# A gated attention + SSM kernel: V's and the gate's weights on GpSimd's DMA queue, and another hand-tuned order

## The chip, the cores and the metric

The kernel runs on one core of a Trainium2 chip. The core has five engines that run their own instruction streams in order and meet at semaphores: TensorE (PE, matrix multiplications), VectorE (DVE), ScalarE (ACT), GpSimd (POOL) and SyncE (SP, here only an issuer of DMAs). ACT and POOL can issue DMAs too; an engine that issues a DMA does nothing else for that long. The metric is the time of one execution in microseconds (us); several executions are made, and the median is taken.

## The reference

Two branches on the same input `x` (2048 tokens of 448 values), mixed by a gate:

```python
g = sigmoid((x * gate_w).sum(-1, keepdims=True))
a = attention(x, wq, wk, wv, wo)     # 16 query heads of 28, ONE key and value head, no mask
b = ssm_conv(x, A_re, A_im, B_re, B_im, C_re, C_im, log_dt, Dskip)
return g * a + (1 - g) * b
```

Attention: `q = x wq` (16 heads of 28), `k = x wk` and `v = x wv` (one head of 28 for all), softmax of `q k^T / sqrt(28)` over all 2048 keys, times `v`, all heads joined times `wo`. That makes 16 x 2048 x 2048 exponentials. The SSM branch builds, for every one of 448 channels, a kernel `K[l] = Re sum_n C dB exp(dt A l)` over 256 complex modes and 2048 places, convolves the channel with it causally, and adds `x * Dskip`. All inputs are bfloat16.

## The kernel before

**Attention.** Queries are worked in 16 units `i` (4 blocks of 512 queries times 4 groups of 4 heads), and each unit has 64 tiles of 128 keys x 512 queries, so there are 1024 tiles. Tiles go in sets of three and two alternately (sets `s`, 410 in all). For each set TensorE computes scores into banks of PSUM (`qk`), ScalarE takes the exponential of the whole set at once (L1357) into a ring `expT` of 15 tiles, and TensorE multiplies four tiles at a time by the values (`pv`, L1383), into the bank `psB`. Scores come in two forms: `row` (L1323) reads `qT`, the query as projected, and puts tiles of different heads in different 32-row groups of the array; `full` (L1332) reads `qM`, a copy of the query with zeros between the heads, which a DMA from POOL's queue writes. Sets below 10, and from 12 on those of three tiles, use the row form. `qproj` projects the next unit's queries, `norm` divides by the softmax's sum, `outp` and `fold` multiply by `wo` and the gate and add into `O`. A shift of the scores keeps the exponentials in range; it comes from the largest key and query magnitudes (`km`, `kap`, `Wb`), so the first score waits for all keys.

**Prologue.** `x` comes in four quarters in the order `QO` = 0, 3, 1, 2. Quarters 0 and 3 are loaded as they are, transposed on TensorE (L718) and copied from PSUM by ACT (L728) or VectorE (L730), as the list `XA` of (quarter, piece) says; quarters 1 and 2 (`DQ`) come in by a transposing DMA, so entries of `XA` for them have no effect. For each quarter four matmuls (L736) make the keys, VectorE takes their largest magnitude (`km`, L742), and the eviction into `kT` is made by VectorE (L746) for quarters in `KD`, else by ACT (L750). V and the gate are one matmul group per 128 tokens (L763) with the weights `Wv`, which VectorE copies (L645, L647) from the staging tile `seedw`; V's and the gate's weights land there by four DMAs of the ACT queue. K's weights and `log_dt` come by the ACT queue too, all others by SP. In the same time ACT and VectorE make the seeds of the SSM tables from A (L862 to L919), for which ACT needs three table loads (exp, sin, exp again).

**SSM branch.** VectorE makes tables (`masters`, `tables`), TensorE makes kernels from them (`kgen`, L1095), VectorE evicts them, POOL's queue writes them to DRAM (`KP`), SP loads them back as Toeplitz tiles (`tload`, L1131), and TensorE convolves (`conv`, L1155), with VectorE (L1170), TensorE (L1181) and VectorE (L1189) adding the result into `O`. There are 28 convolutions. This fills the time of VectorE and what the scores and PV leave of TensorE.

**What sets the order.** The class `Prog` records all operations with an estimated duration, and `schedule` builds the order of each engine's instructions before the kernel is emitted: of the ready operations it takes the earliest, then the one with the smaller `pr`, then the older. Up to the first exponential (`goal`) an operation on a longer path to it goes first, if it makes the other wait for no more than `HEAD` of its duration; `RANK` adds nanoseconds to single operations' path lengths, by number. `ISSUE` is the assumed time of one DMA issue by queue, `extra` an addition to a DMA's assumed landing. An operation with `pr` of 2 or more is assumed ready later by `SLACK`. `idle` puts filler matmuls (L1398, which add zeros into `psB`) into planned gaps of TensorE within the times `FILL`, as long as the planned work of the last `SPAN` ns is below `LOW` of it. Engines run in this order on the chip, whatever arrives first.

## Time and profile before

| | |
|---|---|
| median of 3 runs | 506.75 us (506.19 to 508.49) |
| the profiled execution | 507.17 us, of which the span from first to last instruction is 505.3 us |
| ACT, DVE, PE, POOL busy | 482.6, 455.0, 448.2, 165.3 us |
| exponentials of scores (L1357) | 410, 466.2 us; idle before them 5.8 us |
| first exponential starts | 22.89 us |
| last exponential ends | 495.41 us |
| filler matmuls (L1398) | 36, 0.39 us each, from 40.8 to 392.7 us |
| granted TensorE clock, mean | 0.985 |

In a timeline line the first number is the start in us from the span's start, the second the time taken, then engine, line, operation, tile written, tile read, shapes and count, and in brackets the engine's idle time before it and what ended that. `SPq`, `ACTq` and `POOL ... DMA` lines are issues of DMAs. In a group line the numbers behind the bar are busy time, mean ns of one, and idle time before them with what ended most of it. A line of stretches gives, for a start and an end in us, the length and the busy time and count of PE, PEld, DVE, ACT and POOL, then the granted clock, the DMA engines' busy share and GB/s.

### The profile page before, as it was taken

To read this page: it belongs to the slowest core of one execution; us is meant where nothing else is said; L and a number is where in the kernel's file an instruction comes from. 1 tells how busy PE (TensorE), PEld (TensorE's weight loads), DVE (VectorE), ACT (ScalarE), POOL (GpSimd) and SP (SyncE) were. 2 spreads that over 40 slices of the span, in tenths; PEclk is the share of its full clock that TensorE was granted. 3 is DMA by queue.
4 is the path that set the end of the run, shared out by engine and by line. 5 is a ranking of instruction groups with operands and counts; after the bars stand their busy time and mean duration, and the time that the engine had idled before them with its cause. 6 is when DMAs were issued, how large, how long until landed. Compare 5 with 4: busy or idle time off the path is not lost.

```text
span 505.3 us, 18926 instructions
## 1 busy us (share of the span) xinstructions
PE 448.2 (89%) x8469; PEld 195.1 (39%) x8469; DVE 455.0 (90%) x834; ACT 482.6 (96%) x432; POOL 165.3 (33%) x308
## 2 busy tenths in 40 slices
PE   6797778898998999989898899999899999999885
PEld 2322213343433434334433344344343444344453
DVE  6899999999999999999999999999999999922334
ACT  5899999999999999999999999999999999999892
POOL 8533224252143520615332321435232152451000
PEclk8889999999999999999999999999999999999899
DMA  9977901979949797999989999599999979899982
GB/s 188 224 210 129 59 22 50 340 226 365 363 153 332 244 317 250 269 361 324 366 282 371 318 317 362 199 339 369 356 283 345 369 233 384 264 358 369 385 302 47
DMA packets 123395, 139.51 MB, mean 276 GB/s; under 512 B 56169, under 2 KB 63370, under 8 KB 123314
## 3 DMA queue, kind: packets, MB, share of 16 engines
q1 hardware_dynamic: 112208, 128.89, 79.8%
q0 software_dynamic: 8656, 9.25, 6.7%
q8 instruction: 66, 1.08, 0.9%
q10 hardware_dynamic: 2450, 0.17, 0.4%
q14 instruction: 15, 0.12, 0.1%
HBM read 125.18 MB, written 5.22 MB: 258 GB/s over the span
## 4 chain that ended last, share of the span: by engine, by line
ACT 48%; DVE 38%; PE 10%; issue 2%; DMA 1%; SPq 1%
ACT expT L1357 48%; DVE tab L1048 5%; DVE tab L1059 3%; DVE tab L1060 3%; DVE msq L991 3%; DVE tab L1070 2%; DVE tab L1058 2%; DVE tab L1057 2%; DVE mbf L1011 2%; PE psS L1332 2%; PE psB L1383 2%; DVE seedz L995 2%; PE psS L1323 2%; DVE seedz L993 1%; DVE tmp L1066 1%
## 5 line engine op out<-in xcount | busy, mean ns | idle before, releaser
L1357 ACT ACTIVATE expT<-psS 128x1536 bf16<-128x1536 f32 (+1 forms) x410 | 466.2, 1332 | 5.8 <-PE psS L1323 2.7
L1332 PE MATMUL psS<-qM,kT 128*128 128x512 bf16 (+2 forms) x455 | 122.5, 360 | 13.8 <-ACT expT L1357 10.5
L1383 PE MATMUL psB<-expT,vaug 128*32 128x512 bf16 (+2 forms) x1152 | 103.4, 366 | 3.1 <-issue 2.0
L1323 PE MATMUL psS<-qT,kT 29*128 29x512 bf16 (+2 forms) x699 | 82.1, 362 | 22.9 <-ACT expT L1357 21.5
L154 POOL DMA_DIRECT2D KP_scratch<-kstg x112 | 61.1, 553 | 65.6 <-DVE kstg L1110 37.4
L1048 DVE TENSOR_TENSOR tab<-tab,mbf 128x512 bf16<-128x512 bf16 (+3 forms) x56 | 64.6, 1154 | 0.0
L1383 PEld LDWEIGHTS psB<-expT,vaug 128*32 128x32 bf16 x1152 | 27.6, 93 | 76.1 <-issue 71.2
L154 POOL DMA_DIRECT2D rdenB<-R_scratch x56 | 28.4, 513 | 62.6 <-DMA R_scratch<-denT 53.7
L1332 PEld LDWEIGHTS psS<-qM,kT 128*128 128x128 bf16 x455 | 28.4, 97 | 50.7 <-ACT expT L1357 33.3
L1323 PEld LDWEIGHTS psS<-qT,kT 29*128 29x128 bf16 x699 | 21.4, 91 | 67.4 <-ACT expT L1357 53.6
L154 POOL DMA_DIRECT2D qM<-qT x64 | 32.2, 511 | 37.8 <-DVE qT L966 22.1
L1059 DVE TENSOR_TENSOR tab<-tab 128x1024 bf16<-128x1024 bf16 (+4 forms) x70 | 41.6, 595 | 0.0
L1060 DVE TENSOR_TENSOR tab<-tab 128x128 bf16<-128x128 bf16 (+4 forms) x70 | 41.5, 594 | 0.0
L1155 PE MATMUL psS<-T,U 128*32 128x128 bf16 (+3 forms) x1504 | 35.3, 220 | 0.3 <-DVE qT L966 0.3
L154 POOL DMA_DIRECT2D denT<-acc x14 | 10.0, 715 | 74.8 <-DVE kstg L1106 37.1
L1070 DVE TENSOR_TENSOR tab<-tab,tmp 128x4096 bf16<-128x4096 bf16 x14 | 32.0, 2285 | 0.1
L1058 DVE TENSOR_TENSOR tab<-tab,mbf 128x4096 bf16<-128x4096 bf16 x14 | 31.9, 2279 | 0.0
L1057 DVE TENSOR_TENSOR tab<-tab,mbf 128x4096 bf16<-128x4096 bf16 x14 | 31.9, 2276 | 0.0
L1155 PEld LDWEIGHTS psS<-T,U 128*32 128x32 bf16 (+3 forms) x1504 | 24.9, 94 | 13.8 <-issue 9.4
L1155 PE MATMUL psX<-T,U 128*32 128x128 bf16 (+7 forms) x1216 | 28.8, 222 | 0.1
L991 DVE TENSOR_TENSOR msq<-seedz 128x384 f32<-128x384 f32 (+1 forms) x50 | 27.1, 542 | 0.2
L1066 DVE TENSOR_TENSOR tmp<-tmp,mq 128x64 bf16<-128x64 bf16 (+4 forms) x70 | 25.3, 362 | 0.1
(160 smaller groups left out, 544.2 us busy)
## 6 DMA issues: line engine op xcount, KB each, us to landing
T<-KP_scratch SPq DMA_DIRECT2D x170, 512.0 KB, 9.1
U<-KP_scratch SPq DMA_DIRECT2D x40, 512.0 KB, 9.6
tab<-KP_scratch SPq DMA_DIRECT2D x14, 512.0 KB, 10.9
rdenB<-R_scratch POOLq DMA_DIRECT2D x56, 64.0 KB, 5.5
qM<-qT POOLq DMA_DIRECT2D x64, 32.0 KB, 5.1
tab<-in_A_x_dram SPq DMA_DIRECT2D x8, 224.0 KB, 3.6
O<-cst SPq DMA_DIRECT2D x1, 1792.0 KB, 9.9
KP_scratch<-kstg POOLq DMA_DIRECT2D x112, 16.0 KB, 4.1
```

Of the source, the lines that this page charges most:

```text
L154: return [e.dma_start(o, i, **kw) for o, i in pairs]
L991: pg.op("dve", lambda e: e.tensor_tensor(m2(msq), z2, z2, ALU.mult), el(2 * n), rd=[kr, ki] + first, wr=["msq"], pr=pr)
L1048: vo(lambda e, dst=dst, src=src, mri=mri: e.tensor_tensor(dst, src, mri, ALU.mult), 4 * n, done + mk(lv), [kr, ki, tk])
L1057: vo(lambda e, src=src, mi=mi, tv=tv: e.tensor_tensor(tv, src, mi, ALU.mult), 2 * n, done + mk(lv), [tk])
L1059: vo(lambda e, dc=dc, tc=tc: e.tensor_tensor(dc[0], dc[0], tc[1], ALU.subtract), n, [tk, kr], [kr])
L1060: vo(lambda e, dc=dc, tc=tc: e.tensor_tensor(dc[1], dc[1], tc[0], ALU.add), n, [tk, ki], [ki])
L1070: vo(lambda e: e.tensor_tensor(tab.v(0, P, FM, [[4, 1024], [1, 4]]), tab.v(0, P, lo + 124, [[CG, 32], [-4, 32], [1, 4]]), rho.v(0, P, 0, [ ...
L1155: r = e.matmul(ps.v(32 * j, 32 - 2 * n, 128 * k, [[1, 128]]), self.U.v(0, P, (4 * gi + j) * 32 + 2 * n, [[1, 32 - 2 * n]]), tbuf.v(0, P, t ...
L1323: r = e.matmul(self.psS.v(0, P, 512 * b + o, [[1, n]]), kT.v(32 * h, DH + 1, 128 * kt, [[1, 128]]), qT.v(32 * h, DH + 1, 512 * (i % 2) + q ...
L1332: r = e.matmul(self.psS.v(0, P, 512 * b + o, [[1, n]]), kT.v(0, P, 128 * kt, [[1, 128]]), self.qM.v(0, P, (i % 2) * XQ + 512 * h + qo, [[1 ...
L1357: pg.op("act", lambda e: e.activation(expT.v(0, P, 512 * es[0], spread(es, n)), self.psS.v(0, P, 512 * bs[0], spread(bs, n)), AF.Exp, scal ...
L1383: r = e.matmul(self.psB.v(32 * h, 32, qo, [[1, n]]), vaug.v(0, P, 32 * kt, [[1, 32]]), expT.v(0, P, 512 * ring[t] + o, [[1, n]]), start=(k ...
```

## The change

- V's weights (`wv`) and the gate's (`wg`), two DMAs each, are issued by POOL instead of ACT.
- `XA`: ACT copies pieces 1 and 3 of quarter 0 (before 1, 2, 3) and 0, 1, 2 of quarter 3 (before all four); VectorE copies the rest.
- `KD`: the keys of quarter 2 are evicted by VectorE and those of quarter 1 by ACT (before the other way round).
- Set 10 takes its scores in the row form instead of the full form.
- Numbers of the planner: `HEAD`, `RANK`, the issue time of an ACT DMA, the assumed landing of early, transposing, `wq`, `wv`, `wg` and `kw` DMAs, the fillers' bound `LOW` and last time in `FILL`, the priorities of later query projections (1.5 for 1.58), of the last two convolutions' matmuls (1.3 for 1.6) and of the last units' `norm_last` (0.9 for 1.5 and 2). They issue no instruction; the order of all engines is built from them.

```diff
--- before.py
+++ after.py
@@ -36,8 +36,8 @@
 TW = 4 * 1024
 XQ = NT * 512
 SIN2PI = 6.2831850
-XA = ((0, 1), (0, 2), (0, 3), (1, 0), (2, 2), (2, 3), (3, 0), (3, 1), (3, 2), (3, 3))
-KD = (0, 1, 3)
+XA = ((0, 1), (0, 3), (1, 0), (1, 1), (1, 2), (2, 3), (3, 0), (3, 1), (3, 2))
+KD = (0, 2, 3)
 GX = 3
 DQ = (1, 2)
 VNS = 140
@@ -85,16 +85,16 @@
 class Prog:
     SEM_NS = 56
     DMA_NS = 2200
-    ISSUE = {"pool": 540.0, "sp": 470.0, "act": 470.0}
+    ISSUE = {"pool": 540.0, "sp": 470.0, "act": 700.0}
     LAT = {"pe": 170.0, "act": 173.0, "dve": 82.0, "pool": 85.0, "sp": 60.0}
     SAME = {"act": 100.0, "dve": 125.0, "pool": 150.0}
     SWITCH = 105.0
     BLOCK, FIRST, FETCH, IDLE, NEED = 256, 192, 5900.0, 3300.0, .015
     HALF = (21000.0, 21000.0, 1.8)
-    HEAD = 0.6
-    RANK = {111: 3000, 62: 3000, 39: -6000, 20: -3000, 30: -6000, 190: -6000, 46: -6000, 29: 700, 65: -6000, 84: 6000, 195: 6000, 40: -6000, 38: 3000, 33: 6000}
+    HEAD = 0.4
+    RANK = {111: 3000, 190: -6000, 29: -6000, 38: -6000, 43: 3000, 23: -1500, 41: -3000, 192: -6000, 82: -1500, 153: -6000, 27: -3000, 118: 1500, 37: 1500, 150: -6000, 105: 3000, 39: -6000, 74: -1500, 92: 3000}
     POOL = (7,)
-    LOW, SPAN, FILL = .53, 3413.0, (36000.0, 440000.0)
+    LOW, SPAN, FILL = .45, 3413.0, (36000.0, 490000.0)
     AHEAD = 1500.0
     SLACK = {"pe": 700.0, "dve": 150.0}
 
@@ -157,7 +157,7 @@
         if cost is None:
             cost = nd * ns / 16.0 * (1.15 if size < 1500 else 1.0 if nd >= 512 else 1.4 if size < 3000 else 1.25)
         o = self.op(eng, fn, cost, rd, wr, pr)
-        o.slot, o.ndma, o.extra = slot, len(pairs), extra + 200 * (early or flip)
+        o.slot, o.ndma, o.extra = slot, len(pairs), extra + 500 * (early or flip)
         o.iss = len(pairs) * (1400.0 if flip else 640.0 if early else self.ISSUE[eng])
         prev = self.slots.get(slot)
         if prev is not None:
@@ -626,12 +626,12 @@
         lx(QO[1])
         lraw(1)
         lraw(0)
-        pg.dma(rows(wst, 0, ins["A_wq"], D), (448, 896), "wq", wr=["wqs"], cost=1500)
+        pg.dma(rows(wst, 0, ins["A_wq"], D), (448, 896), "wq", wr=["wqs"], cost=1500, extra=300)
         lx(QO[2])
         lx(QO[3])
-        pg.dma(rows(wks, 4 * DH, ins["A_wv"], DH), (448, 56), "wv", wr=["wvs"], eng="act", cost=150)
+        pg.dma(rows(wks, 4 * DH, ins["A_wv"], DH), (448, 56), "wv", wr=["wvs"], eng="pool", cost=150, extra=2500)
         pg.dma([(wks.v(0, P, 8 * DH, [[2, 3]]), dram(ins["gate_w"], 0, [[1, P], [P, 3]])),
-                (wks.v(0, 64, 8 * DH + 6, [[1, 1]]), dram(ins["gate_w"], 384, [[1, 64], [1, 1]]))], (448, 2), "wg", wr=["wgs"], slow=True, eng="act", cost=150)
+                (wks.v(0, 64, 8 * DH + 6, [[1, 1]]), dram(ins["gate_w"], 384, [[1, 64], [1, 1]]))], (448, 2), "wg", wr=["wgs"], slow=True, eng="pool", cost=150, extra=2500)
         for q in DQ:
             lx(q, True)
         pg.op("pool", lambda e: e.tensor_copy(self.Wk.v(0, P, 0, [[32, 16], [1, DH]]),
@@ -949,7 +949,7 @@
         G = self.grp()
         px = lambda: G.v(0, P, 0, [[1, 512]])
 
-        pr = 0.2 if i == 0 else 1.58
+        pr = 0.2 if i == 0 else 1.5
         for T in range(NT):
             pg.op("pe", lambda e, T=T: e.matmul(
                 px(), self.Wq.v(0, P, T * 512 + g * 128, [[1, 128]]),
@@ -1112,7 +1112,7 @@
         for q in range(2):
             lst = [(dram(self.KP, (32 * c + 16 * q + 4 * g) * KW, [[64, 32], [KW, 4], [1, 64]]),
                     ko.v(32 * g, 32, 256 * q, [[64, 4], [1, 64]])) for g in range(4)]
-            pg.dma(lst, (512, 128), f"kw{q}", rd=["kst", "ksk"], wr=[("KP", c, q)], pr=0, eng="pool", extra=1800)
+            pg.dma(lst, (512, 128), f"kw{q}", rd=["kst", "ksk"], wr=[("KP", c, q)], pr=0, eng="pool", extra=1200)
 
     def tbufs(self):
         n = NC * 8
@@ -1160,7 +1160,7 @@
                 first = k == 0 and n == 0
                 ps.conv[1] = len(pg.ops)
                 o = pg.op("pe", mm, 56, mode="c", ni=8, rd=[("TL", gi), ("Uc", c)] + ([("U", q) for q in range(4)] if c == 0 else []),
-                      wr=[X] + ([("cst", cs)] if first else []), pr=(1.6, 1.6)[c > 25],
+                      wr=[X] + ([("cst", cs)] if first else []), pr=(1.6, 1.3)[c > 25],
                       lock=ps if first else None)
                 if n == 7:
                     o.tfree = tls[k]
@@ -1170,7 +1170,7 @@
         pg.op("dve", lambda e: e.tensor_tensor(self.cst.v(0, P, cs * 512, [[128, 4], [64, 2], [1, 64]]),
                                                ps.v(0, P, 63, [[128, 4], [64, 2], [-1, 64]]),
                                                self.omq.v(0, P, 0, [[0, 4], [64, 2], [1, 64]]), ALU.mult),
-              el(512), rd=[X, "omq"], wr=[("cst", cs), X], pr=2)
+              el(512), rd=[X, "omq"], wr=[("cst", cs), X], pr=(2, 2)[c > 25])
         Y = ("yx", c)
 
         def yt(e, k):
@@ -1187,7 +1187,7 @@
             pg.op("pe", lambda e, k=k: yt(e, k), 70, mode="h", ni=8, rd=[("cst", cs), "id"], wr=[Y], pr=1.55)
         ov = self.O.v(0, P, 15 * D + 16 * c, [[-D, 16], [1, 16]])
         pg.op("dve", lambda e: e.tensor_tensor(ov, ov, px.v(0, P, 0, [[1, 16], [16, 16]]), ALU.add),
-              el(256), rd=[Y], comm=tuple(("O" if c < 26 else "Oz", q) for q in range(7)), pr=2, unlock=px)
+              el(256), rd=[Y], comm=tuple(("O" if c < 26 else "Oz", q) for q in range(7)), pr=(2, 2)[c > 25], unlock=px)
 
     def outp(self, qc, tt):
         pg = self.pg
@@ -1235,7 +1235,7 @@
         hv, rv, on = w(self.acc, 512 * (i % 2)), w(self.rdenB, 0), w(self.onT, 512 * (i % 4))
         ak = [("acc", i % 2, o) if o else ("acc", i % 2)]
         if bank is None:
-            G, pe, dve = self.grp(), 1.5, 2
+            G, pe, dve = self.grp(), 0.9, 0.9
             bc, bk = lambda: G.v(0, P, 0, [[1, n]]), [("bx", i, o)]
         else:
             G, pe, dve = None, 0, 0
@@ -1335,7 +1335,7 @@
                 return r
             if s == 1:
                 pg.after[self.p2] = len(pg.ops)
-            if s < 10 or 12 <= s < 411 and len(ts) == 3:
+            if s < 10 or 9 <= s < 411 and len(ts) == 3:
                 rd = set()
                 for t in ts:
                     i, h, parts = dec(t)
```

## The prediction

> **What bounds the kernel now.** I read the page's busy table first, then the chain that ended last, then ScalarE's waits, then the first 32 us and the last 35 us as a timeline.
>
> ```profile
> PE 448.2 (89%) x8469; PEld 195.1 (39%) x8469; DVE 455.0 (90%) x834; ACT 482.6 (96%) x432; POOL 165.3 (33%) x308
> ACT expT L1357 48%; DVE tab L1048 5%; DVE tab L1059 3%; DVE tab L1060 3%; DVE msq L991 3%; DVE tab L1070 2%; DVE tab L1058 2%; DVE tab L1057 2%; DVE mbf L1011 2%; PE psS L1332 2%; PE psB L1383 2%; DVE seedz L995 2%; PE psS L1323 2%; DVE seedz L993 1%; DVE tmp L1066 1%
> L1357 ACT ACTIVATE expT<-psS 128x1536 bf16<-128x1536 f32 (+1 forms) x410 | 466.2, 1332 | 5.8 <-PE psS L1323 2.7
> ```
>
> ScalarE (ACT) is the bound: 410 exponentials take 466.2 us and are preceded by only 5.8 us of idle. The end is therefore the start of the first exponential, plus 466.2, plus the idle and other work among them, plus what follows the last one. VectorE's 90% is no second bound at the end: its steady work ends near 460 (the page's slices), and the last exponential near 495. The change can move the start, the 5.8 us and the tail. The timeline of ACT at the start, and of the engines that feed it:
>
> ```profile
> 1.38 1.02 ACTq L154 DMA_DIRECT2D seedw<-in_A_wk_dram  x2
> 2.44 1.31 ACTq L154 DMA_DIRECT2D seedw<-in_A_wv_dram  x2
> 3.77 1.30 ACTq L154 DMA_DIRECT2D seedw<-in_gate_w_dram  x2
> 5.10 1.28 ACT L862 ACT_TABLE_LOAD   x1 [5.10 <-issue]
> ...
> 8.89 1.14 DVE L888 TENSOR_TENSOR T<-T,cst 128x896 f32<-128x896 bf16 x1 [0.85 <-DMA T<-in_B_A_re_dram]
> ...
> 10.06 0.95 ACT L891 ACTIVATE T<-T 128x896 f32<-128x896 f32 x1 [0.29 <-DVE T L888]
> ...
> 13.44 1.06 ACT L728 ACTIVATE O<-psS 128x512 bf16<-128x512 f32 x2
> ...
> 15.92 0.60 ACT L728 ACTIVATE O<-psS 128x512 bf16<-128x512 f32 x1 [1.42 <-PE psS L718]
> ...
> 17.40 1.03 PE L736 MATMUL psS<-O,expT 128*128 128x512 bf16 x4
> ...
> 21.59 1.28 ACT L911 ACT_TABLE_LOAD   x1
> ...
> 22.89 1.45 ACT L1357 ACTIVATE expT<-psS 128x1536 bf16<-128x1536 f32 x1
> 24.24 0.68 ACT L750 ACTIVATE kT<-psS,small 128x512 bf16<-128x512 f32 x1
> ```
>
> Four DMA issues keep ACT's queue busy from 2.44 to 5.07, so its first table load starts at 5.10. After A_re lands at 8.89, three copies of x and a wait of 1.42 us stand among the exponentials and sines of the seeds. Two chains meet at 22.89: ACT's own (its last table load ends at 22.87) and keys, bound, query and scores (PE's first L1323 at 22.02). Both have to shorten. The late part of ACT:
>
> ```profile
> 475.80 3.28 ACT L1357 ACTIVATE expT<-psS 128x1024 bf16<-128x1024 f32 x3 [0.81 <-PE psS L1332]
> 479.91 3.71 ACT L1357 ACTIVATE expT<-psS 128x1536 bf16<-128x1536 f32 x3 [0.83 <-PE psS L1323]
> 473.43:476.84 3.41, 1.87 (x46) 0.98 (x42) 0.00 (x0) 2.60 (x4) 0.00 (x0) 1.00 1.04 383
> 477.00:480.30 3.30, 3.30 (x68) 2.14 (x67) 0.00 (x0) 2.47 (x3) 0.00 (x0) 0.50 1.05 384
> ```
>
> The last two lines are stretches of time (PE, PEld, DVE, ACT, POOL busy, granted clock, DMA). PE sat 1.29 us on "issue" at 474.1, that stretch held only 1.87 us of PE work, and the next ran at half clock (0.50): together 1.64 us of ACT idle.
>
> **The change part by part.**
>
> *V's and the gate's weights.* Four issues leave ACT: its table load can start at 2.44 instead of 5.10, 2.66 us earlier. The exponential behind it needs the row at 3.46 + 0.55 = 4.01, so ACT is free for copies at about 5.2 instead of 7.45. POOL gets four issues. No row has POOL issuing 384 pieces of 56 or 2 bytes; POOL's 266 other issues take 0.496 to 0.928 us (the 128-piece KP writes 0.548). I take 0.55, 2.2 us in all, with 2.0 and 3.7 as ends. Behind them in POOL's queue wait the memsets of qM and Wm, the Wk copy (which sits at 5.25 anyhow) and the U copies; the cover is POOL's 4.75 us of idle before the qM DMA at 22.27. With the cover gone, qM would land late, but its first reader is at 35.49. The data land 1.7 to 7.7 us after a POOL issue, at worst at about 4.5 + 7.7 = 12.2; Wv's matmuls (L763) start at 23.53, so that is hidden unless VectorE waits for it (a rival below). The Trainium skill, page "SBUF — State Buffer", section "A bandwidth-pool intuition that's wrong (but worth ruling out)", has a GpSimd-issued DMA go from about 620 to about 3100 ns beside a VectorE tensor_copy; four of these would be 12.4 us by that page. The trace, with VectorE 90% busy, has none above 0.93.
>
> *Copies of x (XA).* Only quarters 0 and 3 are copied. ACT does 7 of 8 now and 5 after; pieces T2 of quarter 0 and T3 of quarter 3 go to VectorE (0.69 each). VectorE is idle for 2.3 of the 5 us from 5 to 10, which hides the first; the second may stand before 8.89 and delay L888 by up to 0.69. With ACT free at 5.2 and T2 copied at 5.6 instead of 7.45, both quarters can be done by about 10.4.
>
> *ACT's chain after.* From L891 at 10.06: five L894 at 0.87 apart, table load 1.28, two sines at 0.97, table load 1.28, with no copy between: the first exponential at 19.9 (3.0 earlier: two copies 1.06, the wait 1.42 and the third copy 0.5). With one copy left over, 20.45.
>
> *The key chain after.* SP's order of loads gets no new instruction; quarter 2's second transposing DMA is issued at 12.1 and lands 3.9 to 4.4 later, near 16.3. Four L736 (1.03): 17.4 instead of 18.43, since the copies no longer hold quarter 3's keys back. From 18.43 to 22.89 the trace has 4.46 us; the needed steps alone (L742 0.65, L775 0.35, L963 0.39, L966 0.65, scores 0.4, hand-overs) are about 2.6, the rest being other VectorE work in its queue. So the first exponential is between 17.4 + 2.6 = 20.0 and 17.4 + 4.46 = 21.9: a gain of 1.0 to 2.9. I take 20.9, 2.0 earlier, nearest to the middle because the order is new and VectorE still has both kinds of work.
>
> *Keys' eviction (KD).* Quarter 1 goes to ACT, quarter 2 to VectorE. Quarter 1 is ready near 15, so its 0.68 on ACT can fit before the first exponential, while ACT waits for the key chain; now it stands behind the first one and costs 0.56 (24.24 to 24.80). Ends 0 and -0.56; I take -0.56.
>
> *Set 10 by row form.* Three L1332 (0.82 together, at 35.49) become one packed group (0.39). PE waits for ACT there: nothing.
>
> *Planner numbers* (HEAD, RANK, ISSUE, the extras, qproj's and conv's priorities) issue nothing themselves; the kw extra reorders the T loads. They redraw the 2.6 us of stalls between 200 and 420 and the 1.64 late: 0, with -2 to +2.
>
> *Fewer fillers (LOW .53 to .45), allowed until 490.* 36 fillers run now, 0.39 each, in PE's idle time, most of them between 40 and 123 us, where ACT doesn't wait: their going gains nothing. Their loss may cost the clock (rival). Taken 0.
>
> *Tail.* 9.87 us after the last exponential (495.41). conv 27 runs on PE from 497.04 to 499.07, and the last add ends at 500.83 while the last fold could end at 499.95: at best -0.9; a conv later by the 1.7 us that a half-clock stretch takes from PE: +1.7. The eager norm_last moves work of the same size about: 0.
>
> Sum: -2.0 - 0.56 = -2.56. The profiled run took 507.17 (span 505.3, 1.87 around it), so 504.6; it lies 0.42 above the median 506.75, which becomes **504.2**.
>
> **The rivals.**
>
> *The ring eats it.* exp writes a ring of 15 tiles; the seventh exponential waits 0.61 us for the first PV at 31.28, which waits for vaug (27.45), in VectorE's queue. If that stays where it is, the wait grows by up to 2.0: 506.2. Against it: VectorE's work before it is the same that delays the first exponential, and should move with it.
>
> *VectorE waits for wv.* If its copy of Wv stands before L888 and the data land at 12.2, ACT's chain slips 3.3 from 19.9 to 23.2: 507.1 at most. For: it already waits 1.31 us for wv at 7.63.
>
> *Slower: fewer fillers drop the clock.* Place: 40 to 100 us, where PE has mostly scores and PV. Stretches of 3.41 us with 1.87 us of PE work lost the clock, those with 2.23 (480.26) and 2.28 (224.28) kept it; those with fillers hold 2.4 to 2.7, so two fillers fewer in one reach the unknown zone. Price 0.49 (26.3 to 29.7, where ACT waited 0.27 + 0.22 at clock 0.50) to 0.83 each. Three stretches at 0.83 eat the gain, seven make it slower; eight give 510.8. By the Trainium skill ("TensorE: Matmul & The Clock Gate", section "HAM oscillation — how this bites in real kernels") only PE-idle gaps above some 3.4 us drop the clock, which would make this rival nothing; the stretch at 473.43 contradicts it, as its longest gap was 1.29.
>
> *The late pair comes again, or goes.* A second "issue" stall with its half-clock stretch: 1.64 on ACT and 1.7 in the tail, 507.5; two, 510.9. Without any: 504.2 - 1.64 - 0.9 = 501.7.
>
> *POOL starved.* Only if each of the four issues took over 2.6 us would the Wk copy pass 12.5 and hold the keys: at 3.1, Wk at 15.3 and 16 L736 at 0.26 end at 19.4 instead of 17.4: 506.2. The highest row is 0.93.
>
> **How the numbers follow.** Forecast 0.40 (its own range 503.3 to 505.2), late pair gone 0.14, ring or wv wait 0.14, fillers 0.14, late pair again 0.15, POOL 0.03. A measurement can tell about 0.5%, 2.5 us: below 504.2 or above 509.3. Faster: 0.26 of the forecast and the 0.14, so 0.40. Slower: 0.09 of the fillers (seven stretches or more) and 0.11 of the late case, 0.20. Same: the rest, 0.40. The range runs from 501.7 (late pair gone) to 509.3, which leaves out the far ends of the fillers and of two late pairs and what lies below: under 0.2.
>
> **What would show it.** Right: ACT's first table load near 2.5, five L728 on ACT and none after 11, L750 before the first exponential, that one at 20 to 21.9, POOL's four issues at 0.55. Wrong: idle before the seventh exponential above 0.6, VectorE idle on wv before L888, granted clock 0.5 between 40 and 470, ACT idle in the last 40 us above 1.7, or more than 9.9 us behind the last exponential.

## The result and the profile after

The kernel after takes 505.54 us (median of 21 executions, 503.3 to 507.68) beside 506.80 us for the kernel before (21 executions, 505.22 to 510.09). The ratio is 0.9967, with a 95% interval from 0.9951 to 0.9983: 0.33% faster by the ratio, and the medians lie 1.3 us apart. That is not no change, but it is inside the 0.5% that the prediction called "same". The forecast was 504.2 us: 505.54 is inside the stated range and just outside the forecast's own, 503.3 to 505.2.

The profiled execution of the kernel after took 506.66 us, with a span of 504.4 us. The page's busy table, and the group of the exponentials:

```profile
PE 426.0 (84%) x8348; PEld 193.9 (38%) x8455; DVE 457.5 (91%) x836; ACT 480.7 (95%) x430; POOL 168.6 (33%) x312
L1357 ACT ACTIVATE expT<-psS 128x1536 bf16<-128x1536 f32 (+1 forms) x410 | 465.4, 1361 | 5.2 <-PE psS L1332 2.7
```

ScalarE is still the bound, with 410 exponentials that now take 465.4 us (466.2 before) and wait 5.2 us (5.8). Part of the matmul records is missing here (8348 beside 8455 weight loads), so PE's busy time is not to be compared with that of before. The start as a timeline:

```profile
1.42 1.44 POOL L154 DMA_DIRECT2D seedw<-in_A_wv_dram  x2 [0.21 <-issue]
2.42 1.28 ACT L862 ACT_TABLE_LOAD   x1 [2.42 <-issue]
2.98 0.29 POOL L542 TENSOR_SCALAR_AFFINE_SELECT ident<-ident 128x128 bf16<-128x128 bf16 x1
3.32 1.46 PE L554 MATMUL psS<-ident 128*128 128x512 bf16 x3 [3.32 <-POOL ident L542]
3.37 1.33 POOL L154 DMA_DIRECT2D seedw<-in_gate_w_dram  x2
...
8.09 0.60 ACT L728 ACTIVATE xT<-psS 128x512 bf16<-128x512 f32 x1 [1.63 <-PE psS L718]
10.35 0.95 ACT L891 ACTIVATE T<-T 128x896 f32<-128x896 f32 x1
13.35 0.61 PE L736 MATMUL psS<-T,expT 128*128 128x512 bf16 x1 [2.08 <-DMA T<-in_A_x_dram]
17.44 1.03 PE L736 MATMUL psS<-O,expT 128*128 128x512 bf16 x4
18.78 0.67 ACT L750 ACTIVATE kT<-psS,small 128x512 bf16<-128x512 f32 x1
20.30 1.28 ACT L911 ACT_TABLE_LOAD   x1
22.50 1.45 ACT L1357 ACTIVATE expT<-psS 128x1536 bf16<-128x1536 f32 x1 [0.92 <-PE psS L1323]
```

And a stretch of time in it (start and end, length, busy time of PE, PEld, DVE, ACT and POOL, granted clock, DMA share, GB/s):

```profile
13.19:16.61 3.42, 3.00 (x10) 1.34 (x12) 2.92 (x5) 3.39 (x5) 3.11 (x6) 0.50 1.07 191
```

ACT's first table load starts at 2.42 instead of 5.10, and the key eviction L750 is out of the way at 18.78. But ACT gains nothing by it: the first exponential waits 0.92 us for scores and starts at 22.50 instead of 22.89. In the stretch the granted clock is 0.50 while TensorE makes the keys of the quarters that came last. The end, TensorE's lines:

```profile
492.47 0.35 PE L1383 MATMUL psB<-expT,vaug 128*32 128x128 bf16 x12
493.86 0.24 PE L1383 MATMUL psB<-expT,vaug 128*32 128x128 bf16 x4 [1.05 <-issue]
495.10 0.57 PE L1155 MATMUL psX<-tab,U 128*30 128x128 bf16 x28
495.50 0.62 PE L1155 MATMUL psS<-tab,U 128*32 128x128 bf16 x32
```

The last exponential ends at 492.16 (495.41 before), and 12.24 us follow it (9.89). TensorE stops 1.05 us on "issue" in the middle of the very last PV group, and then still owes 28 matmuls of convolution 26 and all 128 of convolution 27; before, only those of 27 were left there.

So between the two profiled executions the start gave 0.39 us, the stretch from the first to the last exponential 2.86 us (472.52 to 469.66), and the tail took 2.35 us back: 0.9 us of span.

### The profile page after: what moved, and what is told of

It is laid out like the page before. It is cut to its first block, busy times and chain, and to the rows that moved or that the text cites. A ratio compares the mean times of both kernels' runs of the same rounds, so it can differ in the third digit from the quotient of the medians.

```text
span 504.4 us, 18792 instructions
## 1 busy us (share of the span) xinstructions
PE 426.0 (84%) x8348; PEld 193.9 (38%) x8455; DVE 457.5 (91%) x836; ACT 480.7 (95%) x430; POOL 168.6 (33%) x312
## 3 DMA queue, kind: packets, MB, share of 16 engines
q8 instruction: 66, 1.08, 0.9%
## 4 chain that ended last, share of the span: by engine, by line
ACT 63%; DVE 23%; PE 9%; issue 2%; SPq 2%; DMA 1%
ACT expT L1357 63%; DVE tab L1048 4%; DVE tab L1059 2%; DVE tab L1060 2%; DVE tab L1070 2%; PE psS L1332 2%; DVE tab L1057 2%; DVE tab L1058 2%; PE psS L1323 2%; PE psB L1383 1%; DVE msq L991 1%; DVE tmp L1066 1%; DVE cst L1170 1%; DMA T<-in_A_x_dram 1%; SPq L153 1%
## 5 line engine op out<-in xcount | busy, mean ns | idle before, releaser
L1357 ACT ACTIVATE expT<-psS 128x1536 bf16<-128x1536 f32 (+1 forms) x410 | 465.4, 1361 | 5.2 <-PE psS L1332 2.7
L1332 PE MATMUL psS<-qM,kT 128*128 128x512 bf16 (+2 forms) x358 | 101.7, 356 | 30.6 <-ACT expT L1357 18.0
L1059 DVE TENSOR_TENSOR tab<-tab 128x128 bf16<-128x128 bf16 (+4 forms) x70 | 41.8, 597 | 0.0
L1060 DVE TENSOR_TENSOR tab<-tab 128x128 bf16<-128x128 bf16 (+4 forms) x70 | 41.6, 594 | 0.0
L1155 PE MATMUL psX<-T,U 128*32 128x128 bf16 (+7 forms) x1408 | 33.8, 220 | 0.3
L1155 PE MATMUL psS<-T,U 128*32 128x128 bf16 (+7 forms) x1312 | 32.0, 220 | 1.1 <-issue 0.7
L1095 PE MATMUL psS<-tab 128*32 128x64 bf16 x1280 | 30.2, 242 | 0.8 <-DVE tab L1075 0.7
L1155 PEld LDWEIGHTS psX<-T,U 128*32 128x32 bf16 (+7 forms) x1408 | 24.5, 94 | 14.0 <-issue 9.6
L1095 PEld LDWEIGHTS psS<-tab 128*32 128x32 bf16 x1280 | 23.4, 117 | 12.3 <-issue 7.1
```

What stands on the lines that cost most here:

```text
L1059: vo(lambda e, dc=dc, tc=tc: e.tensor_tensor(dc[0], dc[0], tc[1], ALU.subtract), n, [tk, kr], [kr])
L1060: vo(lambda e, dc=dc, tc=tc: e.tensor_tensor(dc[1], dc[1], tc[0], ALU.add), n, [tk, ki], [ki])
L1095: r = e.matmul(G.v(32 * g, 32, 256 * q + 64 * k, [[1, 64]]), tab.v(0, P, so, [[4, 32]]), tab.v(0, P, fo, [[mo - fo, 2], [4, 32]]), start=( ...
L1155: r = e.matmul(ps.v(32 * j, 32 - 2 * n, 128 * k, [[1, 128]]), self.U.v(0, P, (4 * gi + j) * 32 + 2 * n, [[1, 32 - 2 * n]]), tbuf.v(0, P, t ...
L1332: r = e.matmul(self.psS.v(0, P, 512 * b + o, [[1, n]]), kT.v(0, P, 128 * kt, [[1, 128]]), self.qM.v(0, P, (i % 2) * XQ + 512 * h + qo, [[1 ...
L1357: pg.op("act", lambda e: e.activation(expT.v(0, P, 512 * es[0], spread(es, n)), self.psS.v(0, P, 512 * bs[0], spread(bs, n)), AF.Exp, scal ...
```

## The experiments

All runs but c3, which is told below, with the ratio to the kernel before on the same chip. The runs were made on several chips, and the kernel before has medians from 506.40 to 507.27 us on them, so kernels of different chips are compared by their ratios. From each profile come the start of the first exponential, the end of the last, what follows it in the span (the span to 0.1 us, less the column before), and the sum of TensorE's idle times of 0.2 us or more from 24 us on that end on "issue". The profiles of after, c1, c2 and c4 lack 107 matmul records each; a missing one can look like a stop of 0.2 us, so their sums are somewhat too large:

| kernel | median us | ratio, 95% interval | first exp | last ends | behind it | "issue" stops |
|---|---|---|---|---|---|---|
| before | 506.80 | 1 | 22.89 | 495.41 | 9.89 | 5.45 |
| after | 505.54 | 0.9967 (0.9951 to 0.9983) | 22.50 | 492.16 | 12.24 | 6.03 |
| a0_again | 505.68 | 0.9967 (0.9942 to 0.9993) | 23.01 | 492.49 | 10.41 | 4.60 |
| a1_act | 505.33 | 0.9963 (0.9937 to 0.9989) | 22.56 | 490.56 | 12.04 | 3.83 |
| a2_swap | 506.06 | 0.9987 (0.9962 to 1.0012) | 22.39 | 492.68 | 11.32 | 5.03 |
| a3_warm | 505.88 | 0.9976 (0.9948 to 1.0003) | 21.24 | 492.96 | 10.74 | 5.92 |
| b1_pool | 509.34 | 1.0057 (1.0032 to 1.0082) | 23.16 | 498.38 | 9.62 | 4.94 |
| b2_tail | 507.70 | 1.0030 (0.9999 to 1.0061) | 21.42 | 493.10 | 12.10 | 3.44 |
| b3_fill | 509.70 | 1.0079 (1.0046 to 1.0113) | 21.55 | 495.25 | 10.95 | 11.00 |
| b4_half | 501.87 | 0.9920 (0.9892 to 0.9947) | 21.63 | 487.88 | 10.32 | 0 |
| c1_bhalf | 503.46 | 0.9930 (0.9906 to 0.9953) | 21.93 | 490.91 | 9.89 | 1.35 |
| c2_tailhalf | 502.54 | 0.9910 (0.9888 to 0.9932) | 21.32 | 488.17 | 11.93 | 0.89 |
| c4_warmhalf | 502.22 | 0.9907 (0.9882 to 0.9932) | 21.45 | 490.05 | 10.35 | 4.75 |

The kernels keep the planner's order and move or repeat single operations in it: `move(pg, what, ref)` puts operations right behind operation `ref`, and the waits are then worked out anew.

**The same kernel again (a0).** No edit.

> The changed kernel once more, nothing edited. Its first profile had the first exponential at 22.50 us, a half-clock stretch of 10.2 us from 39.8 with 1.33 us of ScalarE idle in it, and 12.2 us behind the last exponential, with a 1.05 us stop of TensorE ahead of the last PV. If these belong to the order, they come again: first exponential within 0.1 of 22.50, a half-clock stretch between 38 and 50, more than 11 us behind the last exponential. If they were chance, the clock holds between 38 and 50 or the tail is near 10 us, while the first exponential stays.

505.68 us: the ratio is the same. Its profile is not: the clock is not halved between 38 and 51 us (the profile of the kernel after has it halved from 40.5 to 50.7, with 1.33 us of ACT idle), the first exponential is at 23.01 (the last of quarter 1's load lands at 14.16, in the profile of after at 13.31), and its longest late stop of TensorE is at 481.20 (1.30 us) and not at 493.86. So half-clock stretches and the places of late stops are not properties of the order alone, and one profile of each kernel is not enough to put a gain of 1.3 us down to them.

**V's and the gate's weights back on ACT's queue (a1).** Operations 57 and 58 are their DMAs, 50 is that of K's weights.

```diff
+    for i in (57, 58):
+        pg.ops[i].eng = 'act'
+    move(pg, [57, 58], 50)
```

> The changed kernel in its own order, with V's and the gate's four loads issued by ScalarE again, behind K's weights, as in the kernel before. Theory (keys and VectorE set the first exponential, ScalarE waits 0.92 us for them): ScalarE's first table load moves from 2.42 to about 5.1, identity and the first transposes of x come up to 1 us earlier, and the first exponential stays within 0.4 of 22.50. Rival (ScalarE's queue is the bound, and the move to GpSimd bought the gain): first exponential 1 to 2 us later, at 23.5 or beyond.

```profile
5.09 1.28 ACT L862 ACT_TABLE_LOAD   x1 [5.09 <-issue]
20.03 1.28 ACT L911 ACT_TABLE_LOAD   x1
22.56 3.71 ACT L1357 ACTIVATE expT<-psS 128x1536 bf16<-128x1536 f32 x3 [1.25 <-PE psS L1323]
```

ACT's table load is back at 5.09, and nothing else moves: the first exponential still waits for scores (1.25 us), the time is 505.33. In the new order no gain or loss of the queue that issues these four DMAs can be measured.

**Only wv's place in POOL's queue (a2).** Its DMA goes behind the affine select that finishes the identity, so that TensorE's first product no longer waits for two issues.

```diff
+    move(pg, [57], 3)
```

> The changed kernel with V's two loads moved one place down in GpSimd's queue, behind the operation that finishes the identity matrix. Rival theory (the two issues at 1.42 to 2.86, ahead of the identity, delay TensorE's first work from 1.63 to 3.32 and ate the gain): TensorE starts near 1.7, the first transposes of x at 5.0 instead of 6.0, and the first exponential is 1 us or more earlier, 21.5 or below. Theory (the keys of quarters 1 and 2, whose loads land at 13.3 and later, and VectorE behind them set it): TensorE and ScalarE start earlier, the first exponential moves by less than 0.4.

L891 comes at 9.71 instead of 10.35 and ACT's last table load at 19.65 instead of 20.30; the first exponential at 22.39, after a wait of 1.46 us. All that ACT gains it waits longer. 506.06 us. ACT's first copy of x shows how little the identity held: its finishing select ends at 1.58 here, ACT is free at 4.88, and the copy still comes at 7.51, after a wait of 2.63 us (8.09 in the kernel after, 7.45 in the one before). TensorE's first product of x starts at 5.47, released by the load of x, and VectorE takes the first two pieces.

**TensorE kept busy in its wait for quarter 1 (a3).** Nine products of the identity where the order has one, moved to where TensorE waits for that quarter's load.

```diff
+    f = pg.ops[91].fn
+    pg.ops[91].fn = lambda e: [f(e) for _ in range(9)][-1]
+    move(pg, [91], 95)
```

> The changed kernel with nine matmuls of the identity (512 columns each) in the 2.1 us that TensorE waits for quarter 1 of x, from 11.3 to 13.35; two of its idle-time matmuls before that are taken into them. Theory (TensorE at half clock from 13.1 to 16.5 while it makes the keys, then VectorE): the clock holds from 13 to 16.5, the keys' largest-value reductions on VectorE start near 16.1 instead of 16.78, and the first exponential comes 0.4 to 0.8 earlier, near 21.9. Rival (the load of quarter 2 or VectorE alone set it): the clock holds, and the first exponential stays within 0.2 of 22.50.

```profile
16.16 1.03 PE L736 MATMUL psS<-O,expT 128*128 128x512 bf16 x4
21.24 1.45 ACT L1357 ACTIVATE expT<-psS 128x1536 bf16<-128x1536 f32 x1 [0.38 <-PE psS L1323]
```

The clock stays at 1.00, the last keys are made at 16.16 instead of 17.44, and the first exponential starts 1.26 us earlier than in the profile of the kernel after, more than the 0.4 to 0.8 expected. The time does not follow: 505.88 us. Between 60 and 300 us ACT waits 3.5 us here (0.6 there).

**The queue's edit alone, in the order of before (b1).** The order of before; wv's DMA behind the identity's affine select, the gate's behind the next memset.

```diff
+    for i in (57, 58):
+        pg.ops[i].eng = 'pool'
+    move(pg, [57], 3)
+    move(pg, [58], 18)
```

> The kernel before in its own order, with one edit: V's two loads and the gate's two are issued by GpSimd, right behind the operation that finishes the identity and the memset after it. Theory (keys and VectorE set the first exponential): ScalarE's first table load moves from 5.10 to about 2.5, the copies of quarter 0 come up to 2 us earlier, but the first exponential moves by less than 0.5 from 22.89, and the time stays within 0.25%. Rival (this edit is what the change gained): first exponential 1 us or more earlier and the time at least 1 us below before.

509.34 us, 0.57% slower than before, which neither expectation had. Its timeline:

```profile
8.23 7.00 POOL L668 COPY U<-tab 128x896 bf16<-128x896 bf16 x4
12.25 1.10 DVE L639 COPY Wq<-mbf 128x448 bf16<-128x448 bf16 x1
24.85 2.43 POOL L668 COPY U<-tab 128x896 bf16<-128x896 bf16 x2
24.91 1.47 DVE L919 SCALAR_TENSOR_TENSOR seedz<-T 128x448 f32<-128x448 f32 x1
26.31 1.92 DVE L888 TENSOR_TENSOR mbf<-T,cst 128x896 f32<-128x896 bf16 x1
29.69 0.61 DVE L788 CAST vaug<-psB 128x448 bf16<-128x448 f32 x1
30.34 0.18 ACT L793 ACTIVATE gt<-psB 128x16 f32<-128x16 f32 x1 [0.64 <-DVE vaug L788]
45.45 0.77 PE L830 MATMUL psS<-acc,onT 16*128 16x64 f32 x5 [1.48 <-DVE acc L824]
46.64 4.69 ACT L1357 ACTIVATE expT<-psS 128x1536 bf16<-128x1536 f32 x4 [1.40 <-PE psS L830]
```

and the stretch behind it, at half clock:

```profile
47.38:57.62 10.24, 9.47 (x42) 2.04 (x38) 8.00 (x35) 8.73 (x8) 0.00 (x0) 0.50 0.76 54
```

The second pair of copies of U in the kernel before:

```profile
24.38 0.62 DVE L919 SCALAR_TENSOR_TENSOR seedz<-T 128x448 f32<-128x448 f32 x1
24.41 5.85 POOL L668 COPY U<-tab 128x896 bf16<-128x896 bf16 x2
24.91 1.08 DVE L888 TENSOR_TENSOR mbf<-T,cst 128x896 f32<-128x896 bf16 x1
```

POOL's four copies of U, which stand behind the issues, run from 8.23 to 15.23 (before: 5.87 to 10.92) and so lie beside other work of VectorE: L639 takes 1.10 us (0.35 before). Two more copies of U start at 24.85, hardly later than before (24.41). There it is the other way round than before: in the kernel before POOL's two copies take 5.85 us, the first of them 4.00, and VectorE's L919 and L888 beside it are short (0.62, 1.08); in b1 the two copies take 2.43 us and VectorE's two are longer, 1.47 and 1.92. V's cast is 2.24 us later than before (29.69 for 27.45), and 1.69 of that are these two instructions, which do not lie beside the four delayed copies. VectorE's copy L824 is 1.08 us later (45.13 for 44.05), and L830 waits for that copy; TensorE idles 1.48, ACT 1.40, and TensorE runs at half clock from 47.4 to 57.6; ACT waits 2.1 us more until 58.3. The first to last exponential takes 475.22 us, 2.70 more than before. That is read from one profile; whether the loss needs the delay of the four copies was to be shown by c3.

**POOL's fills behind the copies of U, in b1 (c3).** Nine fills of POOL moved, and POOL's operations linked anew, each to the one before it.

```diff
+    move(pg, [29, 20, 21, 22, 23, 24, 25, 37, 38], 81)
+    p = [i for i in pg.seq if pg.ops[i].eng == 'pool']
...
+        pg.ops[b].deps[a] = 1
```

> b1 (the order of before, wv and the gate's weights issued by GpSimd) with nine of GpSimd's fills (two of qM, five and a larger one of the mask and onT with its affine select, 2.6 us together) moved behind its four copies of U, so that these start near 5.7 again as in the kernel before (5.87; 8.23 in b1). b1 took 509.34, its profile has VectorE's copies of 0.35 to 1.08 us at 0.75 to 0.85 us more beside GpSimd's copies, the cast of V 2.2 us later, ScalarE idle 0.64 for the gate, and TensorE idle 1.48 for VectorE's copy at L824 with half clock behind it (46.7 to 56.9). Theory 1 (GpSimd's delay of 2.4 us is what costs): V's cast back near 27.5, no wait of ScalarE above 0.3 at L793, 506 to 507. Theory 2 (the delay of the identity and of TensorE's start, or the transfers themselves): 508.5 to 510, the wait at L830 as in b1.

```profile
1.89 1.47 POOL L154 DMA_DIRECT2D seedw<-in_A_wv_dram  x2 [0.31 <-POOL ident L542]
6.40 0.10 POOL L536 MEMSET seedw<- 64x1 bf16 x1 [3.03 <-DMA seedw<-in_A_wv_dram]
6.79 1.31 POOL L154 DMA_DIRECT2D seedw<-in_gate_w_dram  x2 [0.29 <-POOL seedw L536]
11.82 0.47 POOL L536 MEMSET mbf<- 64x448 bf16 x1 [3.73 <-DMA seedw<-in_gate_w_dram]
```

630.59 us. The edit did more than it should: the new links hold for DMAs too, so POOL waits for the landing of each of its own transfers before its next instruction, 3 to 4 us each time, all through the kernel. The run answers another question (what it costs to make the issuing queue wait: 120 us here) and leaves the one on b1 open.

**The old priorities of the tail (b2).**

```diff
-            G, pe, dve = self.grp(), 0.9, 0.9
+            G, pe, dve = self.grp(), 1.5, 2
-                      wr=[X] + ([("cst", cs)] if first else []), pr=(1.6, 1.3)[c > 25],
+                      wr=[X] + ([("cst", cs)] if first else []), pr=(1.6, 1.6)[c > 25],
```

> The changed kernel with the priorities of the kernel before for the last units' normalisation and the last two convolutions; the order is the same up to the last 16 us of exponentials. Theory (after the last exponential TensorE still owes 156 convolution matmuls and a fetch stop, whatever the priorities): more than 10.3 us behind the last exponential and the time within 0.7 us of the changed kernel's 505.6. Rival (the new priorities push the convolutions back): under 10 us behind the last exponential, and the time 1 us or more lower.

507.70 us, by the ratios (1.0030 and 0.9967) 0.6% above the kernel after. What follows the last exponential, 12.10 us, is as expected; the time, which was to stay within 0.7 us, is not. In its profile the stop of TensorE is at 478.98 (1.17 us), half clock follows from 480.4 to 490.7, and ACT waits 3.3 us from 470 to 500 (0.4 in the profile of after).

**Twenty filler matmuls more between 31 and 48 us (b3).** Two behind each of ten PV groups.

```diff
+    for i in (257, 263, 266, 272, 278, 282, 288, 291, 297, 303):
+        pg.fill[i] = pg.fill.get(i, 0) + 2
```

> The changed kernel with 20 more filler matmuls, two behind each of ten PV groups from 31 to 48 us. They also move every 256th-instruction mark of TensorE's stream back by 20 matmuls, so that the last mark before the end stands behind the last scores instead of inside the last PV. Theory: the clock holds from 30 to 60 and ScalarE idles 0.3 or less there (0.3 to 1.3 in the two profiles of the changed kernel); the 0.4 to 1.2 us stop at the last PV goes or falls beside the last exponentials, and the time is 0.5 to 1.2 us lower. Rival (fillers hold the scores up, or the stops lie elsewhere): ScalarE idles more than 0.6 between 30 and 60, or the time is not lower.

509.70 us, by the ratios 1.1% slower than after, although the clock is 1.00 from 9 to 502 us. The three largest of TensorE's waits on "issue" in the stretch from 60 to 445 us, of this kernel (us in all, times, longest):

```profile
PE psS L1155 <- issue: 3.3, 3, 1.6
PE psX L1155 <- issue: 3.3, 4, 1.5
PE psS L1095 <- issue: 1.4, 2, 0.9
```

Its waits on "issue" there are 8.5 us (3.7 in the profile of after), the longest 1.65 at 285.5, after which ACT waits 0.77. From 60 to 500 us ACT waits 6.8 us (2.4). Twenty matmuls are forty instructions, so every later stop falls at another place in the work; why there are more and longer ones than in the other orders the run doesn't say.

**Half of each Toeplitz load from the thirteenth convolution on (b4).** The kernel leaves out 512 of the 1024 columns wherever the buffer was once loaded whole, so the later convolutions are not computed rightly; the engines' instructions stay.

```diff
+            w = 512 if gi >= 48 and tl.home in FULL else 1024
+            FULL.add(tl.home)
-            return [e.dma_start(bass.AP(tensor=buf.h, offset=h * buf.rs + o, ap=[[2 * buf.rs, 64], [1024, 4], [1, 1024]]),
-                                dram(self.KP, h * 1024 + 4 * gi * KW, [[1, 64], [KW, 4], [1, 1024]])) for h in range(2)]
+            return [e.dma_start(bass.AP(tensor=buf.h, offset=h * buf.rs + o, ap=[[2 * buf.rs, 64], [1024, 4], [1, w]]),
+                                dram(self.KP, h * 1024 + 4 * gi * KW, [[1, 64], [KW, 4], [1, w]])) for h in range(2)]
```

> The changed kernel, but from the 13th convolution on SP loads only half of each row of the Toeplitz tiles (512 of 1024 columns) wherever that buffer was once loaded whole; the other half is left from earlier, so the convolutions are wrong, and all engines do the same work. Theory (the loads, with the DMA engines busy at 1.05 until 490, hold the last two convolutions back until the scores and PV no longer leave room for them): the loads end before 475, convolutions 26 and 27 are done or nearly done at the last exponential, less than 9.6 us follow it, and TensorE's stops for instructions shrink; the time is 2 us or more lower. Rival (TensorE's own work sets the tail): more than 10.5 us behind the last exponential, the time within 1 us of 505.6.

501.87 us. By the ratios (0.9920 and 0.9967) that is 0.5%, some 2.4 us, below the kernel after, with TensorE's instructions unchanged. The stretch from 445 to 490 us in the kernel after:

```profile
445.00:490.00 45.00, 39.88 (x954) 22.40 (x960) 16.63 (x23) 44.43 (x40) 6.36 (x12) 1.00 1.05 376
```

and in b4:

```profile
445.00:490.00 45.00, 41.58 (x1010) 23.16 (x1006) 15.97 (x22) 42.71 (x39) 6.37 (x12) 1.00 0.72 222
```

The only line on "issue" among TensorE's waits of b4 from 60 to 500 us (in all, times, longest):

```profile
PE psB L1385 <- issue: 0.2, 1, 0.2
```

The DMA engines' busy share falls from 1.05 to 0.72, and the stops, 6.03 us in the profile of after, are gone; the exponentials wait 1.6 us in all instead of 5.2.

**The half loads with the order of before (c1), with the old tail (c2), with a3's products (c4).** The edits of b4 added to the kernel before, to b2 and to a3; these kernels leave out the same columns.

> The kernel before, with b4's halved loads: from the group of rows 48 on, only 512 of the 1024 columns of a Toeplitz row are loaded into a buffer that was loaded whole before, so the later convolutions are computed from stale columns. b4, the same on the kernel after, took 501.87 us against 505.5, and no stop of TensorE on its own instructions of 0.2 us or more is left in its profile (10 before that, 6.0 us together). Theory 1 (the gain of the change is in where those stops fall: 0.81 + 0.83 us of ScalarE's idle time at 474 to 480 in the kernel before): without the stops the two kernels are level: 501.5 to 502.3. Theory 2 (the gain is in the start and the stream: the key eviction ahead of the first exponential, 0.56, the first exponential itself 0.4 to 1.5 earlier): the distance of 1.3 stays or grows: 503 to 504. Rival (the loads cost this kernel nothing): 506.4 to 506.8.

> The kernel after with b2's old priorities of the tail and b4's halved loads (the same columns left out of the later convolutions). b2 alone took 507.7, some 2 us above the kernel after; its profile has a stop of 1.17 us of TensorE at 479.0, half clock from 479.7 to 489.9, and ScalarE idle 3.3 us between 470 and 500 (0.4 in the profile of the kernel after). Theory 1 (the old tail costs by where the stops fall and by the clock that drops behind them): without the stops level with b4, 501.5 to 502.5. Theory 2 (the old order of the last work is longer by itself): 503.5 to 504.5.

> The kernel after with a3's nine products of the identity in TensorE's wait for the second quarter of x and b4's halved loads (the same columns left out of the later convolutions). a3 alone had its first exponential at 21.24 (after: 22.50 and 23.01) and no gain in time (505.88). Theory 1 (what the early start gained was lost to TensorE's stops on its own instructions, 5.1 us of them between 60 and 445): without the stops an early first exponential reaches the end: about 1 us below b4's 501.87 if b4's first exponential is at 22.5, 501.0 to 501.9 since b4's stood at 21.63 in its profile. Theory 2 (something behind the stream, the last convolutions or their loads, sets the end): 501.9 to 502.5, with the time behind the last exponential longer than b4's by what the start is earlier.

503.46, 502.54 and 502.22 us on one chip. The old tail, 0.6% slower than the new one with whole loads, is as fast with half loads (0.9910, b4 0.9920), so its cost goes with the loads, and is not more work. The order of before stays 0.9 and 1.2 us behind the two others, about the 1.3 of the whole loads, though the intervals overlap. The kernel that differs from it by the change alone is b4, made on another chip: 0.9930 beside 0.9920, about 0.5 us and well inside both intervals. So c1 leaves open whether the gain stays without the stops. Its profile still has L750 behind the first exponential (0.56) and a wait of 1.1 us for the first PV (at half clock), which no profile with the new order has. c4 was to show an early start reach the end and can't: its first exponential is at 21.45 where b4's was already at 21.63. Its stops were not gone either (4.75 us, 3.37 of them before 445, the longest 1.04); so half loads make stops fewer and not always none.

## Why the prediction was right in direction, and where its steps failed

The faster side held, the gain was 1.3 us and not 2.56. That the total came this near is in part luck: between the two profiles the stretch of exponentials gained 2.3 us that the sum had at 0, the tail lost 2.35 where it had 0, and the start gave 0.39 where it had 2.0.

- **Key chain, first exponential 2.0 us earlier: the step that failed.** It came 0.39 earlier in the two profiles. The step took the last four key matmuls from 18.43 to 17.4 because copies would no longer hold them back. What held them was the clock. In the six profiles where the last keys end at 18.4 or later (before, after, a0, a1, a2, b1) TensorE ran at half clock from 13.6 at the latest to 16.1 or longer; in the five without it and without a3's products (c1 with the order of before; b2, b3, b4, c2 with that of after) they end at 17.3 to 17.5. The last load of x lands no earlier there, at 15.9 to 16.4 (15.8 to 16.5 in the six), so it isn't that. a3, whose products keep the clock up, has them at 17.2. In the five the order of before has its first exponential at 21.93, that of after at 21.32 to 21.63. So the order is worth 0.3 to 0.6 us, and the clock in that stretch about 1 (22.89 to 21.93 with the order of before). The rest of the chain, 4.46 us in the profile of before, was taken as 3.5 and is 4.03 in after (18.47 to 22.50) and 4.08 in b2: VectorE's list of L742, L746, L768, L774, L960 and L775 stands there in order whatever ACT does.

From the timeline of b2, the same start as in after with the clock at full speed:

```profile
16.31 1.03 PE L736 MATMUL psS<-O,expT 128*128 128x512 bf16 x4
...
21.42 3.71 ACT L1357 ACTIVATE expT<-psS 128x1536 bf16<-128x1536 f32 x3
```

- **V's and the gate's weights: ACT's part right, POOL's part short.** The table load came at 2.42 as forecast (2.44). The issues took 0.72 and 0.67 us each, not 0.55, within the ends given. The step named the memsets and the U copies behind them and left out the identity: its affine select now ends at 3.27, and TensorE starts at 3.32 instead of 1.63. ACT waits 1.59 us for a product of TensorE (L854) at 5.30 and then, free at 6.46, 1.63 us for its first copy of x at 8.09. The identity is only part of that: in a2, which has it early, the copy comes at 7.51, so some 0.6 us are the identity's, and the rest of the gain of 2.66 us is spent on waiting for x and for VectorE's copies of the first two pieces, where the step had the copy at 5.6. L891 came at 10.35, later than before. a1 and a2 show that it would not have counted: ACT's chain is not the one that ends last.
- **ACT's chain (19.9 us): too early by 1.7** (its last table load ends at 21.58), for the reason just given and since two L728 stand behind L891 (11.21, 13.36), where the step had none, or one at most.
- **Copies of x on VectorE "hidden": right as far as is known.** VectorE's idle time from 5 to 22 us fell from 4.0 to 1.6 us. Its first L888 took 1.90 us instead of 1.14, and L891 lost about 0.3 by that; but this L888 starts at 8.41 beside POOL's copies of U (from 8.34), and in a2, with the same copies of x, it starts at 7.95, just ahead of them (8.02), and takes 1.09. So, by these two profiles, the copies of x are not what lengthened it.
- **Keys' eviction: right,** 0.56: L750 at 18.78, the first three exponentials without a gap.
- **Planner numbers, 0 with 2 either way:** the stretch between first and last exponential is 2.86 us shorter, 2.3 beyond the eviction. About 1.5 of that are waits of ACT, the rest shorter exponentials. It lies just past the end given, on the good side.
- **Tail, 0 with ends -0.9 and +1.7:** 9.89 us became 12.24, 10.41 in the second profile of the same kernel. The end was too narrow: it priced a later convolution but not a stop inside the last PV with convolution 26 still unfinished.
- **The rivals.** *The ring* is refuted: no exponential waits for the first PV after. *VectorE waits for wv* is refuted: VectorE doesn't wait for it. *Late pair*: ACT's waits from 470 to 500 fell from 1.6 to 0.4 us in one profile and were 1.8 in the other, so it neither goes nor stays with the change. *Fillers* is not borne out as a price: the half clock from 40.5 to 50.7 came in one of two profiles and cost ACT 1.33 us there, and more fillers (b3) made the kernel slower.
- **The clock rule.** In the kernel after, the half clock from 13.2 comes right behind a gap of 2.08 us (11.27 to 13.35), the longest since TensorE's first product at 3.32; the one from 40.5 has no gap above 0.74 us in the 3.4 us ahead of it. In the Trainium skill, page "TensorE: Matmul & The Clock Gate", section "HAM oscillation — how this bites in real kernels", the rule is "no PE-idle gaps >~3.4µs". The runs disagree again. But the bound of PE work by which the prediction priced the rival falls too. The stretch ahead of 40.5 and what followed, in the kernel after and in its second run (a0):

```profile
37.09:40.50 3.41, 2.12 (x14) 0.51 (x13) 3.22 (x8) 3.41 (x4) 0.00 (x0) 1.00 1.01 242
40.50:50.74 10.24, 9.87 (x50) 3.53 (x49) 9.86 (x29) 8.70 (x8) 4.12 (x6) 0.50 0.51 81
37.47:40.88 3.41, 2.12 (x15) 0.51 (x13) 3.25 (x7) 3.41 (x4) 0.00 (x0) 1.00 1.02 244
40.88:44.30 3.42, 3.10 (x27) 1.51 (x25) 3.28 (x11) 3.42 (x4) 2.19 (x5) 1.00 0.75 196
```

The same 2.12 us of recorded PE work lost the clock once and kept it once (a few matmul records are missing in the first). In the kernel before, too, a stretch with 1.85 us (19.50 to 22.91) kept it, and one with 2.59 (22.92 to 26.33) lost it. So the PE work of 3.4 us does not decide alone, and no price per filler follows from it.

What stays open: which of the moves in the new order carries the 1.3 us (the eviction and the missing wait for the first PV are the candidates that the profiles show), and why the queue's edit alone costs 2.9 us in the old order and nothing in the new one. For the second, b1's profile shows longer instructions of VectorE beside POOL's copies and TensorE waiting for VectorE behind them, and no run has isolated it. No kernel that computes the whole result was measurably faster than the kernel after: a1 is 0.2 us lower, well inside its interval.

## What to carry to other kernels

An engine that is relieved gains only until it meets the chain beside it: before a start is priced, find what that other chain waits for, here a load, TensorE's clock and VectorE's list in order. When an instruction is put at the head of a queue, list everything that stands behind it, above all the small operation that another engine's first instruction needs, and what its later start will overlap with. In a kernel whose DMA engines are full, look at stops on "issue": a new order moves them, and an edit worth 1 us can be hidden, or feigned, by where they fall.

## What the runs showed of the hardware

- **TensorE can stop every 256 of its instructions where the DMA engines are full.** From 440 us on, the stops on "issue" stand 128 matmuls and 128 weight loads apart, in the second run of the kernel after at 468.71, 475.00 and 481.20:

```profile
468.71:475.00 6.29, 5.32 (x127) 2.83 (x128) 1.82 (x3) 5.97 (x6) 0.00 (x0) 1.00 1.05 386
475.00:481.20 6.20, 4.79 (x128) 3.37 (x128) 2.56 (x3) 5.43 (x5) 0.00 (x0) 1.00 1.05 385
```

They last 0.2 to 1.65 us, add up to 3.4 to 11 us in the nine profiles with whole loads, and to 0 to 4.75 with half loads. That the load on the DMA engines makes them longer is shown by b4. What TensorE waits for is its next instructions, as the DMA queue of kind "instruction" shows on the page of the kernel after:

```profile
q8 instruction: 66, 1.08, 0.9%
```

These 66 packets are of 16 KB, one for every 256 of TensorE's 16,910 matmuls and weight loads. In the nine profiles with whole loads each of the 73 stops of 0.2 us or more ends 1.2 to 1.6 us after the end of such a packet; in the second run of the kernel after the packets end at 467.29, 473.53 and 479.84 for the three stops named. Those profiles have 66 such packets each, so most packets cause no stop of that length.

- **The granted clock is lost in stretches of 3.4 us or multiples of it** (3.4, 6.8 and 10.2 us in the profiles of the table, up to 17.1 in c3), and two executions of one program can differ in whether one comes: 40.5 to 50.7 in one profile of the kernel after, none there in the other.
- **VectorE beside POOL's copies:** single instructions took 1.8 to 3.1 times their time (L639 1.10 us for 0.35, L888 1.92 for 1.08), others none more. Which side pays changes with the order: at the two copies of U near 24.4 POOL took 4.00 us for the first one in the kernel before, with L919 and L888 beside it at 0.62 and 1.08; in b1 it took 2.43 for both, with these two 1.69 longer. So a copy's row from one order is no price for another.
